# Gate stage's entry: order of token roundings and weight sums; last stage: place of the y and T2 block loads

## The chip, the core and the metric

The kernel runs on one core of a Trainium2 chip. The metric is the device time of one execution in microseconds; for the kernel before, the median of three runs is 1006.84 us (1005.92 to 1007.14). The core has TensorE (PE, matmuls into PSUM), VectorE (DVE), ScalarE (ACT), GpSimd (POOL) and SyncE (SP), whose queue issues most of the DMA transfers. Each engine works through its own queue in order; engines wait for each other with semaphores.

## The reference

`x` is 2048 tokens of 640 features. The result is `x` plus a Fourier mixing of the normalized tokens plus a gated feed-forward layer on them, all in fp32:

```python
xn = _layernorm(x, axis=-1)
a = jnp.einsum("bsd,ed->bse", xn, dft_hid_re)
b = jnp.einsum("bsd,ed->bse", xn, dft_hid_im)
y = jnp.einsum("ts,bse->bte", dft_seq_re, a) - jnp.einsum("ts,bse->bte", dft_seq_im, b)
gate = jnp.einsum("bsd,df->bsf", xn, W_gate)
up = jnp.einsum("bsd,df->bsf", xn, W_up)
gate = gate * (gate > 0)
return x + y + jnp.einsum("bsf,fd->bsd", gate * up, W_down)
```

The hidden width F is 1728, that is 13 tiles of 128 features and 64 left over.

## The kernel before

**Precision.** Every fp32 operand is split into a rounded high part and the low part that is left. `split` (L198) does it: ScalarE rounds (L199), VectorE subtracts (L200). A product is `mm3`, three matmuls one after the other: high by high (L205), high by low (L206), low by high (L207). So the first of three waits for what ScalarE rounded, the second for the token's low part, the third for the weight's low part.

**Three stages.** The first multiplies the sequence DFT with the normalized tokens (`cb` blocks against `xs_early`, `xs_late`) and ends near 399 us. The second is the gate stage: for each of 13 tiles of features it computes gate and up with a fast matrix scheme of 48 products of weight sums and token sums. The last stage, from about 724 us, projects the hidden values and the first stage's result into the output, in two halves `q` of 1024 tokens, `q = 1` first.

**The gate stage** is written as a list of events with keys. `at(key, f)` enters one, the list is sorted by key, and on each engine the instructions stand in that order, by hand. A tile has a period of 33 keys and its products run over 66, so two tiles overlap. Its steps are in `STEPS`: `mm` is a product (weight group, piece, token operand, bank), `seed` has ScalarE copy one PSUM bank into another (L1094), `snap` has it copy a bank to an `ev` buffer (L196), `add` adds a buffer into a bank on VectorE (L1104), `addout` and `both` are likewise VectorE's (L1109, L1115), `final` applies the gate (L1121).

- *Tokens.* 32 token operands are in `FIRST_USE` with the key of their first product. Each is loaded (`fill_slot`, L839) into `mv`, `r` or `xs_early` and split there by `split_slot`: a rounding on ScalarE and directly after it the low part on VectorE, at one key. For the first 14 that key is at most -18 + 1.1 i, for the others 5.5 ahead of the first use. Tokens in `FLIPPED` change sign (L845, L846).
- *Weights.* A tile's raw weights (`gw`, for odd tiles `st`) go through 23 sums, `SUMS`, each one subtraction or addition of 128x128 (L999). `high` then rounds a group of them on ScalarE (L196) and `low` takes the low part on VectorE (L1075). The sums of the first two tiles have fixed keys and are all VectorE's; those of the second start soon after the first tile's products. From the third tile on `plan_sums` places them: at each key where VectorE works on a PSUM bank it gives GpSimd one sum that is free (`sum_beside`, which lets the sum wait for the VectorE instruction just before); a sum that gets due without such a place goes to VectorE.

**The last stage** is a list of units. `B11`, `T1`, `T2`, `B22`, `T3`, `T4` are seven units each, (name, u); `B21` has two. A unit has the steps `load` (token blocks `rw`, `ro`, by `get`), `fetch` (weights `wt`), `prepare` (subtractions L1526, then the split into `cb`), `run` (matmuls) and a reading of the banks; `drive_last` calls them so that loads stand six units ahead of the matmuls, and `prepare` three. SP, POOL and PE keep this order; VectorE and ScalarE are ordered by the scheduler. T1 works on `B12 - B11`, T2 on `B22 - B12`; `load` fetches the `B22` blocks at certain units of T1 and T2. `get_y` loads the input rows `y` (L1433, 256 KB each) to which `add_y` adds a bank (L1438). B11's banks for outputs 0 and 1 are used on by T2, T1's by B22, so they are read in between. In the first half B11's first five units are computed in the gate stage already.

Of the kernel before, what the change touches and what calls it, by code (L numbers as in the profile page):

```python
# [7 lines left out]
F32 = mybir.dt.float32  # L8
F32R = mybir.dt.float32r
AF = mybir.ActivationFunctionType  # L10
# [16 lines left out]
NF = F // P  # L27
# [78 lines left out]
SPLIT_LEAD, FIRST_SPLIT = 5.5, -18  # L106
# [21 lines left out]
def fnet_reglu_kernel(  # L128
# [712 lines left out]
    def split_slot(o):  # L841
        hi, lo = place[o]
        z = lo.bitcast(F32)
        if o in FLIPPED:
            nc.scalar.activation(hi, z, AF.Copy, scale=-1.0)  # L845
            nc.vector.scalar_tensor_tensor(lo, z, -1.0, hi.bitcast(F32), op0=OP.mult, op1=OP.subtract)  # L846
        else:
            split(hi, lo, z)
# [157 lines left out]
    def plan_sums():  # L1006
# [16 lines left out]
        done = {(1, i): max(PERIOD + key, 5 + key / 20) for i, (key, *_) in enumerate(SUMS)}  # L1023

        def free_at(n, i):
            o, _, a, b = SUMS[i][1:]
            t = PERIOD * n - LOADED
# [5 lines left out]
            if n > 1:  # L1033
# [8 lines left out]
        todo = [(n, i) for n in range(2, NF) for i in range(len(SUMS))]  # L1042
# [96 lines left out]
    for n in range(NF):  # L1139
        k0 = PERIOD * n  # L1140
        at(k0 - LOAD_LEAD if n > 1 else -70 + n * 30, load_tile, n)
        for key, *what in SUMS if n < 2 else ():
            at(max(k0 + key, 5 + key / 20) if n == 1 else k0 + key, sum_step, n, *what)
# [77 lines left out]
    for o, (key, s) in zip(combos[UPPER:], places):  # L1221
        at(key, load_again, o, s)
        at(used[o] - SPLIT_LEAD, split_slot, o)
# [187 lines left out]
    Y_AT = {n: "y0" if i < 8 else "y1" if i < 9 else "y2" for i, n in enumerate("001 101 401 41 01 11 21 31 20 30 000 100 400".split())}  # L1411
    HOMES = {"wts": (0,) * 2 + (1,) * 3 + (2,) * (AHEAD - 4), "lead": (1, 0, 0, 1, 1, 2), "low": (0,) + (1,) * 5}
# [39 lines left out]
    def project(q):  # L1452
# [27 lines left out]
        def unit(name, u, first, last):  # L1480
# [7 lines left out]
            def load():  # L1488
# [3 lines left out]
                ahead = {("T1", 2): 0, ("T1", 4): 1, ("T1", 6): 2, ("T2", 0): 3, ("T2", 2): 4, ("T2", 3): 5, ("T2", 4): 6}.get((name, u))  # L1492
# [144 lines left out]
        for name, us in (("B11", every), ("T1", every), ("T2", every), ("B22", every[:4]), ("T3", every), ("B22", every[4:]), ("T4", every)):  # L1637
            for u in us:
# [147 lines left out]
```

## Time and profile before

| | |
|---|---|
| median of three runs | 1006.84 us |
| profiled execution | 1008.12 us |
| its span, first to last instruction | 1006.3 us |
| TensorE matmul | 994.3 us, 4393 |
| VectorE | 884.8 us |
| ScalarE | 526.1 us |
| GpSimd | 146.1 us |
| DMA | 261.14 MB, mean 259 GB/s |
| granted TensorE clock | 1.000 |

An engine's time is the time in which it was busy. Lines of the profile have the form "engine line operation out<-in", L12 being line 12 of the kernel before. A matmul of 128x512 lasts 0.39 us, but the next begins 0.23 us after it, so they overlap, and TensorE counts as busy through short stalls; starts tell more than busy time. In a timeline the brackets at the end give the idle time of the engine ahead of an instruction and what ended it.

### The profile page before, as it was taken

The page shows a single profiled execution, that of the slowest core. Times are in us where ns is not written, and L with a number is a line of the kernel's source. Part 1 is how long each engine was busy: PE and PEld are TensorE (multiplying, and loading weights), DVE is VectorE, ACT ScalarE, POOL GpSimd, SP SyncE. Part 2 cuts the span into 40 slices and gives each one's busy share as a digit, 9 for nine tenths or more (in the row PEclk, how much of TensorE's full clock was granted, in tenths as well). Part 3 has the DMA queues.
Part 4 walks back from the last instruction along what each step waited for, and adds up shares of the span by engine and source line. Part 5 has one row for each costly group of instructions (what it writes and reads, how often), then busy time and mean ns, then how long its engine had stood idle before and what let it go on. Part 6 is the DMA issues. An engine that isn't in the chain of part 4 may idle for free.

```text
span 1006.3 us, 13555 instructions
## 1 busy us (share of the span) xinstructions
PE 994.3 (99%) x4393; PEld 816.8 (81%) x4393; DVE 884.8 (88%) x1462; ACT 526.1 (52%) x832; POOL 146.1 (15%) x285
## 2 busy tenths in 40 slices
PE   9999999999999999999999999999999999999998
PEld 7888888888888888778888888888777888888886
DVE  7968999999989989998999999997778987679877
ACT  6664444333333555776666666657434454444552
POOL 2000000000000000024444544432000001000001
PEclk9999999999999999999999999999999999999999
DMA  9877894986948867716898998765698779999785
GB/s 330 315 256 266 270 326 152 364 303 202 400 140 294 331 200 249 272 66 193 268 263 247 267 255 260 213 179 154 218 398 273 251 251 335 317 308 329 225 273 167
DMA packets 183671, 261.14 MB, mean 259 GB/s; under 512 B 14944, under 2 KB 127200, under 8 KB 183504
## 3 DMA queue, kind: packets, MB, share of 16 engines
q1 hardware_dynamic: 147200, 208.82, 61.6%
q0 software_dynamic: 10944, 38.44, 12.9%
q10 hardware_dynamic: 25456, 13.01, 4.3%
q8 instruction: 34, 0.56, 0.2%
q14 instruction: 37, 0.30, 0.1%
HBM read 198.34 MB, written 75.94 MB: 273 GB/s over the span
## 4 chain that ended last, share of the span: by engine, by line
PE 72%; DVE 11%; issue 8%; DMA 6%; ACT 2%; SPq 1%; POOL 0%; DVEq 0%; ACTq 0%; POOLq 0%
PE ps L205 23%; PE ps L206 23%; PE ps L207 23%; PE ps L583 3%; DVE cb L200 2%; DVE raw L750 1%; DMA pq<-sb 1%; DMA pl<-in_wd 1%; DVE gw L999 1%; DMA rw<-pq 1%; DMA pq<-sa 1%; PE ps L612 1%; DMA rw<-hd 1%; DVE w L1075 1%; PE ps L1585 1%
## 5 line engine op out<-in xcount | busy, mean ns | idle before, releaser
L206 PE MATMUL ps<-cb,wt 128*128 128x512 f32 (+1 forms) x389 | 151.4, 389 | 1.3 <-DVE cb L200 1.2
L205 PE MATMUL ps<-cb,wt 128*128 128x512 f32 (+1 forms) x389 | 151.0, 388 | 1.0 <-ACT cb L199 1.0
L207 PE MATMUL ps<-cb,wt 128*128 128x512 f32 (+1 forms) x389 | 151.0, 388 | 0.0
L199 ACT ACTIVATE cb<-rw 128x1024 fp32r<-128x1024 f32 (+1 forms) x91 | 86.6, 962 | 79.1 <-PE ps L207 42.6
L199 ACT ACTIVATE cb<-raw 128x1024 fp32r<-128x1024 f32 x64 | 67.7, 1060 | 101.6 <-PE ps L207 65.9
L200 DVE TENSOR_TENSOR cb<-rw,cb 128x1024 fp32r<-128x1024 f32 (+1 forms) x91 | 99.4, 1103 | 18.8 <-ACT cb L199 18.0
L206 PE MATMUL ps<-cb,xs_late 128*128 128x512 f32 x232 | 90.5, 390 | 0.1
L1094 ACT ACTIVATE ps<-ps 128x512 f32<-128x512 f32 x104 | 59.2, 581 | 60.0 <-DVE ps L1104 40.3
L200 DVE TENSOR_TENSOR cb<-raw,cb 128x1024 fp32r<-128x1024 f32 x64 | 78.0, 1220 | 14.3 <-ACT cb L199 14.2
L205 PE MATMUL ps<-cb,xs_late 128*128 128x512 f32 x232 | 90.3, 389 | 0.0
L207 PE MATMUL ps<-cb,xs_late 128*128 128x512 f32 x232 | 90.3, 389 | 0.0
L206 PE MATMUL ps<-cb,xs_early 128*128 128x512 f32 x226 | 88.0, 390 | 0.0
L207 PE MATMUL ps<-cb,xs_early 128*128 128x512 f32 x226 | 87.9, 389 | 0.0
L205 PE MATMUL ps<-cb,xs_early 128*128 128x512 f32 x226 | 87.9, 389 | 0.0
L206 PEld LDWEIGHTS ps<-cb,wt 128*128 128x128 f32 x389 | 73.0, 188 | 17.9 <-DVE cb L200 2.9
L196 ACT ACTIVATE ev<-ps 128x512 f32<-128x512 f32 x117 | 69.9, 597 | 33.2 <-PE ps L207 30.3
L205 PEld LDWEIGHTS ps<-cb,wt 128*128 128x128 f32 x389 | 73.0, 188 | 16.5 <-ACT cb L199 1.4
L207 PEld LDWEIGHTS ps<-cb,wt 128*128 128x128 f32 x389 | 73.0, 188 | 14.8
L1109 DVE TENSOR_TENSOR ev<-ps,ev 128x512 f32<-128x512 f32 x91 | 62.4, 686 | 11.8 <-PE ps L207 10.8
L999 POOL TENSOR_TENSOR gw<-gw 128x128 f32<-128x128 f32 x104 | 48.5, 467 | 134.3 <-DVE gw L999 55.1
L199 ACT ACTIVATE wt<-wt 128x768 fp32r<-128x768 f32 (+5 forms) x60 | 38.4, 646 | 54.1 <-DMA wt<-wparts 53.9
L199 ACT ACTIVATE cb<-tk 128x1024 fp32r<-128x1024 f32 x32 | 33.8, 1060 | 50.1 <-DVE tk L750 24.5
(251 smaller groups left out, 2307.9 us busy)
## 6 DMA issues: line engine op xcount, KB each, us to landing
raw<-in_dft SPq DMA_DIRECT2D x94, 512.0 KB, 6.8
wt<-wparts SPq DMA_DIRECT2D x74, 256.0 KB, 4.9
rw<-hd SPq DMA_DIRECT2D x27, 512.0 KB, 6.7
hd<-ev SPq DMA_DIRECT2D x45, 256.0 KB, 3.6
tok<-r ACTq DMA_DIRECT2D x24, 448.0 KB, 6.0
wt<-wparts SPq DMA_DIRECT2D x27, 384.0 KB, 5.3
rw<-pq SPq DMA_DIRECT2D x19, 512.0 KB, 6.0
wparts<-pw SPq DMA_DIRECT2D x24, 384.0 KB, 4.2
```

The costliest lines, as they stand in the source:

```text
L196: return nc.scalar.activation(o, i, AF.Copy)
L199: nc.scalar.activation(hi, src, AF.Copy)
L200: return nc.vector.tensor_tensor(lo, src, hi.bitcast(F32), op=OP.subtract)
L205: nc.tensor.matmul(ps, wh, mh, start=first, stop=False, skip_group_check=more)
L206: nc.tensor.matmul(ps, wh, ml, start=False, stop=False, skip_group_check=more)
L207: nc.tensor.matmul(ps, wl, mh, start=False, stop=last, skip_group_check=more)
L583: nc.tensor.matmul(E[0, key], xn_part(n * SG + j, d)[v == 1], b[:, int(v == 2), j], start=False, stop=n % NH == NH - 1 and (j, v) == (SG - ...
L612: nc.tensor.matmul(E[c, key], xn_part(j, d)[v == 1], b[c][0][:, int(v == 2), j], start=j == 0 and v == 0, stop=False)
L750: sub = lambda o, i0, i1: nc.vector.tensor_tensor(o, i0, i1, op=OP.subtract)
L999: return (engine or nc.vector).tensor_tensor(operand(n, o), operand(n, a), operand(n, b), op=OP.add if op == "+" else OP.subtract)
L1094: nc.scalar.activation(banks[n, x], banks[n, s], AF.Copy, scale=float(sign))
L1109: tt(t, banks[n, x], snaps[n, s], op=OP.add if op == "+" else OP.subtract)
```

## The change

It has three parts. In the gate stage a token's rounding and its low part become two events: `high_slot` stands 2 keys ahead of `low_slot`, and the keys are in a table, `SPLITS`, in place of the rule. The second tile's sums are placed by `plan_sums` too, with the limit that none starts earlier than 28 keys ahead of its tile (38 for later tiles). In the last stage's first half the `B22` blocks are fetched at other units (`ROWS_AHEAD`), B11's banks are read after the last unit of T1 and T1's after the fourth of T2 (`READ_AFTER`), and their y are loaded with T1's last and T2's second unit (`Y_BEFORE`).

```diff
-SPLIT_LEAD, FIRST_SPLIT = 5.5, -18
+SPLITS = {20: -18.5, 38: -18.4, 26: -19.8, 21: -14.7, 22: -15.1, 23: -19.5, 39: -10.9, 28: -14.3, 24: -8.2, 25: -8.1, 42: -7.0, 27: -5.9, 29: -4.3, 30: -3.7, 31: 21.5, 35: 24.5, 32: 26.5, 33: 28.0, 34: 29.5, 36: 34.5, 37: 33.5, 40: 30.5, 41: 37.5, 43: 40.0, 44: 42.5, 45: 46.5, 46: 49.5, 47: 56.5}
+ROUND_AHEAD = 2.0
...
-    def split_slot(o):
+    def high_slot(o):
+        hi, lo = place[o]
+        nc.scalar.activation(hi, lo.bitcast(F32), AF.Copy, scale=-1.0 if o in FLIPPED else 1.0)
+
+    def low_slot(o):
         hi, lo = place[o]
         z = lo.bitcast(F32)
         if o in FLIPPED:
-            nc.scalar.activation(hi, z, AF.Copy, scale=-1.0)
             nc.vector.scalar_tensor_tensor(lo, z, -1.0, hi.bitcast(F32), op0=OP.mult, op1=OP.subtract)
         else:
-            split(hi, lo, z)
+            nc.vector.tensor_tensor(lo, z, hi.bitcast(F32), op=OP.subtract)
...
-        done = {(1, i): max(PERIOD + key, 5 + key / 20) for i, (key, *_) in enumerate(SUMS)}
+        done = {(0, i): key for i, (key, *_) in enumerate(SUMS)}
...
-            t = PERIOD * n - LOADED
+            t = PERIOD * n - (LOADED if n > 1 else 28)
...
-        todo = [(n, i) for n in range(2, NF) for i in range(len(SUMS))]
+        todo = [(n, i) for n in range(1, NF) for i in range(len(SUMS))]
...
-        at(min(used[o] - SPLIT_LEAD, FIRST_SPLIT + 1.1 * i), split_slot, o)
+        at(SPLITS[o] - ROUND_AHEAD, high_slot, o)
+        at(SPLITS[o], low_slot, o)
...
+    ROWS_AHEAD = ({("T1", 2): 0, ("T1", 4): 1, ("T1", 6): 2, ("T2", 0): 3, ("T2", 2): 4, ("T2", 3): 5, ("T2", 4): 6},
+                  {("T1", 3): 0, ("T1", 5): 1, ("T2", 0): 2, ("T2", 1): 3, ("T2", 2): 4, ("T2", 4): 5, ("T2", 5): 6})
+    READ_AFTER = {(1, "B11"): ("T1", 6), (1, "T1"): ("T2", 3)}
+    Y_BEFORE = {(1, "T1", 6): "B11", (1, "T2", 1): "T1"}
...
-                    step.append((l, p, r, (lambda name: lambda: read(name))(kind) if last else idle, f))
-                loaded = "B11" if q and (name, u) == ("T1", 2) else name if u == (5 if q and name == "T1" else 3) and (q, name) != (1, "B11") else None
+                    done = [n for n in ((kind,) if last else ()) if (q, n) not in READ_AFTER] + [n for (k, n), at in READ_AFTER.items() if k == q and at == (kind, i)]
+                    step.append((l, p, r, (lambda names: lambda: [read(n) for n in names])(done), f))
+                loaded = Y_BEFORE.get((q, name, u), name if u == 3 and (q, name) not in READ_AFTER else None)
```

The table for `q = 0` in `ROWS_AHEAD` is the one of before. How instructions move is shown at three places, with the line numbers of each kernel.

**VectorE, from the first tile's products on,** between two adds into a bank (`ps`). `gw<-gw`, `gw<-st` and the like are weight sums, `st` being the second tile's raw weights; `r1` is a token's low part, `w3` and `wb` those of weight groups. Before:

```order
L1104 TENSOR_TENSOR ps_3288<-ps_3288,ev6_3501 128x512
L999 TENSOR_TENSOR gw_3296<-gw_3296,st_3332 128x128
L999 TENSOR_TENSOR gw_3296<-st_3332,gw_3296 128x128
L200 TENSOR_TENSOR r1_2757<-r1_2757 128x512 x2
L999 TENSOR_TENSOR gw_3296<-gw_3296 128x128
L999 TENSOR_TENSOR gw_3296<-gw_3296,st_3332 128x128
L1075 TENSOR_TENSOR wb_3537<-gw_3296,wb_3537 128x384
L999 TENSOR_TENSOR gw_3296<-st_3332 128x128
L1075 TENSOR_TENSOR w3_3546<-gw_3296,w3_3546 128x384
L999 TENSOR_TENSOR gw_3296<-st_3382,st_3332 128x128
L999 TENSOR_TENSOR gw_3296<-gw_3296 128x128
L1104 TENSOR_TENSOR ps_3291<-ps_3291,ev2_3563 128x512
```

The same piece of the changed kernel:

```order
L1112 TENSOR_TENSOR ps_3288<-ps_3288,ev6_3496 128x512
L852 TENSOR_TENSOR r1_2757<-r1_2757 128x512 x2
L1007 TENSOR_TENSOR gw_3296<-gw_3296,st_3332 128x128
L1007 TENSOR_TENSOR gw_3296<-st_3332,gw_3296 128x128
L1007 TENSOR_TENSOR gw_3296<-st_3332,st_3383 128x128
L1083 TENSOR_TENSOR wb_3529<-gw_3296,wb_3529 128x384
L1083 TENSOR_TENSOR w3_3538<-gw_3296,w3_3538 128x384
L1007 TENSOR_TENSOR gw_3296<-st_3332 128x128
L1112 TENSOR_TENSOR ps_3291<-ps_3291,ev2_3553 128x512
```

Seven sums stand between the adds before and four now. Back to the low part of the first tile's second weight group it is 18 and 7; from the second add to the next such add, 3 and 7. Of the second tile's 23 sums, nine are GpSimd's now and 14 VectorE's; of the third tile's, GpSimd has 13 in place of 19.

**ScalarE, right behind,** from the copy `ev2` that the second add above reads to the copy `ev3` of another bank. `ps<-ps` are seeds, the second of which reads the bank of that add; `r1` are token roundings, `w3` and `w1` weight roundings. Before:

```order
L196 ACTIVATE ev2_3563<-ps_3288 128x512
L1094 ACTIVATE ps_3292<-ps_3287 128x512
L1094 ACTIVATE ps_3289<-ps_3291 128x512
L199 ACTIVATE r1_2757<-r1_2757 128x512
L1174 ACTIVATE ev4_3585<-ps_3293 64x512
L196 ACTIVATE w3_3595<-gw_3296 128x384
L196 ACTIVATE w1_3600<-gw_3296 128x128
L199 ACTIVATE r1_2757<-r1_2757 128x512
L196 ACTIVATE ev1_3606<-ps_3287 128x512
L196 ACTIVATE w3_3608<-gw_3296 128x384
L199 ACTIVATE r1_2757<-r1_2757 128x512
L196 ACTIVATE ev3_3616<-ps_3289 128x512
```

The same piece of the changed kernel:

```order
L197 ACTIVATE ev2_3553<-ps_3288 128x512
L844 ACTIVATE r1_2757<-r1_2757 128x512
L1102 ACTIVATE ps_3292<-ps_3287 128x512
L1102 ACTIVATE ps_3289<-ps_3291 128x512
L1182 ACTIVATE ev4_3580<-ps_3293 64x512
L844 ACTIVATE r1_2757<-r1_2757 128x512
L197 ACTIVATE w3_3593<-gw_3296 128x384
L197 ACTIVATE w1_3598<-gw_3296 128x128
L844 ACTIVATE r1_2757<-r1_2757 128x512
L197 ACTIVATE ev1_3604<-ps_3287 128x512
L197 ACTIVATE w3_3606<-gw_3296 128x384
L197 ACTIVATE ev3_3612<-ps_3289 128x512
```

Three roundings stand between the second seed and `ev3` before, two now, and one stands ahead of the seeds. Further on, one rounding fewer stands ahead of the seed for the second tile's product at key 45. At the stage's start ten token roundings stand ahead of the first weight rounding in place of eight.

**SP, in the last stage's first half,** from the loads for T1's fourth unit on (`rw<-hd1` pairs and `ro` are token blocks, `rw<-pq3` of 128x1024 is a `B22` block, `wt` weights). Before:

```order
L1433 DMA y001_6878<-in_xt 128x512
L1433 DMA y101_6880<-in_xt 128x512
L1433 DMA y41_6882<-in_xt 128x512
L1433 DMA y401_6884<-in_xt 128x512
L1504 DMA wt_6892<-wparts_96 128x2x384
L1476 DMA rw_6894<-hd1_93 128x2x512
L1476 DMA rw_6896<-hd1_93 128x2x512
L1504 DMA wt_6922<-wparts_96 128x384
L1472 DMA ro_6924<-hd1_93 128x512
L1474 DMA rw_6926<-pq3_91 128x1024
L1472 DMA ro_6928<-hd1_93 128x512
L1504 DMA wt_6948<-wparts_96 128x2x384
```

The changed kernel:

```order
L1518 DMA wt_6876<-wparts_96 128x2x384
L1490 DMA rw_6878<-hd1_93 128x2x512
L1488 DMA rw_6880<-pq3_91 128x1024
L1490 DMA rw_6882<-hd1_93 128x2x512
L1518 DMA wt_6890<-wparts_96 128x384
L1486 DMA ro_6892<-hd1_93 128x512
L1486 DMA ro_6894<-hd1_93 128x512
L1518 DMA wt_6920<-wparts_96 128x2x384
L1490 DMA rw_6922<-hd1_93 128x2x512
L1488 DMA rw_6924<-pq3_91 128x1024
L1518 DMA wt_6950<-wparts_96 128x2x384
L1490 DMA rw_6952<-hd1_93 128x2x512
```

The four y stood ahead of all of this, with the first `B22` block; two more y stood ahead of the loads for T1's last unit. Now the four follow behind the last row shown, and the two behind T2's first weights and blocks. On VectorE the four adds to these y stand behind the preparation of T1's last unit and T2's first two, where before they stood ahead of T1's fourth unit; the first matmul of T2 waits for one of them and its seventh for another.

More of the change, by code (lines that the diff above doesn't have):

```diff
@@ L1141, in fnet_reglu_kernel @@
         at(k0 - LOAD_LEAD if n > 1 else -70 + n * 30, load_tile, n)
-        for key, *what in SUMS if n < 2 else ():
-            at(max(k0 + key, 5 + key / 20) if n == 1 else k0 + key, sum_step, n, *what)
+        for key, *what in SUMS if n < 1 else ():
+            at(k0 + key, sum_step, n, *what)
         for g, what in enumerate(WEIGHTS):
@@ L1222, in fnet_reglu_kernel @@
         at(key, load_again, o, s)
-        at(used[o] - SPLIT_LEAD, split_slot, o)
+        at(SPLITS[o] - ROUND_AHEAD, high_slot, o)
+        at(SPLITS[o], low_slot, o)
     assert len(places) >= len(combos) - UPPER, (len(places), len(combos))
@@ L1491, in load @@
                     get(kind, u)
-                ahead = {("T1", 2): 0, ("T1", 4): 1, ("T1", 6): 2, ("T2", 0): 3, ("T2", 2): 4, ("T2", 3): 5, ("T2", 4): 6}.get((name, u))
+                ahead = ROWS_AHEAD[q].get((name, u))
                 if ahead is not None:
```

5 lines of the change are left out of this document (4 added, 1 removed).

## Prediction

> **What bounds the kernel now.** I read the page first, then stretches of 50 us, then who waited for whom on TensorE, then the timeline at the waits.
>
> ```profile
> PE 994.3 (99%) x4393; PEld 816.8 (81%) x4393; DVE 884.8 (88%) x1462; ACT 526.1 (52%) x832; POOL 146.1 (15%) x285
> 400.00:450.00 50.00, 47.44 (x200) 36.54 (x199) 46.71 (x105) 37.55 (x75) 4.97 (x11) 1.00 0.50 171
> 600.00:650.00 50.00, 50.00 (x221) 41.22 (x220) 46.69 (x114) 33.60 (x69) 23.27 (x46) 1.00 0.87 241
> 700.00:750.00 50.00, 47.86 (x208) 38.37 (x207) 37.17 (x53) 20.31 (x32) 2.72 (x5) 1.00 0.78 283
> 750.00:800.00 50.00, 49.55 (x218) 40.39 (x217) 45.17 (x52) 24.25 (x31) 0.00 (x0) 1.00 0.82 271
> ```
>
> TensorE is busy 99% of the span, at a granted clock of 1.00 (the third figure from the end of a stretch). A stretch that waits for nothing holds 221 matmuls in 50 us, one every 0.226 us. The change adds and removes no matmul, so it can only win stalls. They lie where the count falls short: 200 in the stretch in which the gate stage begins (21 short, 4.7 us), 208 and 218 where the last stage begins (16 short, 3.6 us). That is the ceiling, some 8 us of 1006.
>
> ```profile
> PE ps L205 <- ACT ev L196: 1.4, 1, 1.4
> PE ps L205 <- ACT ps L1094: 1.2, 3, 0.7
> PE ps L206 <- DVE cb L200: 1.2, 2, 0.8
> PE ps L205 <- ACT cb L199: 1.0, 1, 1.0
> PE ps L205 <- DVE ps L1115: 0.6, 2, 0.3
> ```
>
> The releasers are ScalarE and VectorE: a bank's copy (L196) and seed (L1094), an add into a bank (L1115), and in the last stage the two halves of a token block (L199, L200). At the places themselves (start, duration, matmul):
>
> ```profile
> 425.28 0.39 PE L207 MATMUL ps<-mv,w 128*128 128x512 f32 x1
> 427.04 0.50 PE L205 MATMUL ps<-r,w 128*128 128x512 f32 x1 [1.38 <-ACT ev L196]
> 427.38 0.40 PE L206 MATMUL ps<-r,w 128*128 128x512 f32 x1
> 429.67 0.39 PE L207 MATMUL ps<-r,w 128*128 128x512 f32 x1
> 430.76 0.50 PE L205 MATMUL ps<-r,wa 128*128 128x512 f32 x1 [0.71 <-ACT ps L1094]
> 439.53 0.39 PE L207 MATMUL ps<-mv,w 128*128 128x512 f32 x1
> 439.89 0.50 PE L205 MATMUL ps<-mv,w 128*128 128x512 f32 x1
> 441.85 0.40 PE L207 MATMUL ps<-mv,w 128*128 128x512 f32 x1
> 442.55 0.50 PE L205 MATMUL ps<-xs_early,w 128*128 128x512 f32 x1 [0.31 <-DVE ps L1115]
> ...
> 746.27 0.39 PE L207 MATMUL ps<-cb,wt 128*128 128x512 f32 x1
> 747.68 0.51 PE L205 MATMUL ps<-cb,wt 128*128 128x512 f32 x1 [1.02 <-ACT cb L199]
> 748.94 0.50 PE L206 MATMUL ps<-cb,wt 128*128 128x512 f32 x1 [0.75 <-DVE cb L200]
> 754.97 0.39 PE L205 MATMUL ps<-cb,wt 128*128 128x512 f32 x1
> 755.75 0.50 PE L206 MATMUL ps<-cb,wt 128*128 128x512 f32 x1 [0.40 <-DVE cb L200]
> 759.74 0.39 PE L205 MATMUL ps<-cb,wt 128*128 128x512 f32 x1
> 760.17 0.50 PE L206 MATMUL ps<-cb,wt 128*128 128x512 f32 x1
> ```
>
> A stall costs start minus the start before, less 0.23, and 0.11 more because the matmul after a restart follows at 0.34 (427.04 to 427.38). So in the gate entry 1.53, 0.86, 0.13 and 0.47, and 0.11 each: **3.4 us** in four stalls. In the last stage 1.18, 1.03, 0.55, 0.20 and three times 0.11: **3.3 us**.
>
> **The gate entry, part by part.** Rows of ScalarE and VectorE ahead of the stall of 1.53 us:
>
> ```profile
> 419.55 0.60 ACT L196 ACTIVATE ev<-ps 128x512 f32<-128x512 f32 x1
> 422.08 0.58 ACT L1094 ACTIVATE ps<-ps 128x512 f32<-128x512 f32 x1 [1.19 <-DVE ps L1104]
> 426.40 0.59 ACT L196 ACTIVATE ev<-ps 128x512 f32<-128x512 f32 x1
> 426.88 1.15 ACT L199 ACTIVATE r<-r 128x512 fp32r<-128x512 f32 x2
> ...
> 421.35 0.69 DVE L1104 TENSOR_TENSOR ps<-ps,ev 128x512 f32<-128x512 f32 x1
> 429.34 0.69 DVE L1104 TENSOR_TENSOR ps<-ps,ev 128x512 f32<-128x512 f32 x1
> 447.08 0.48 DVE L999 TENSOR_TENSOR gw<-gw 128x128 f32<-128x128 f32 x2
> ```
>
> TensorE waits for the copy at 426.40, ScalarE stood idle 1.19 us for the add at 421.35, and that add stood behind VectorE's sums. A sum takes VectorE 0.20 us (a second one makes 0.48 of 0.28). Between the low part of the second weight group and this add stand 18 sums before and 7 now (the second tile's other sums come later or go to GpSimd): 11 x 0.20 = 2.2 us less, which would put the add at 419.15. Its other input, the copy at 419.55, is ready at 420.15, so the add starts there, 1.2 us sooner. ScalarE now puts a token's rounding (0.52 each: two in 1.15) into the idle time, and the two seeds follow; the second can start at 420.15 + 0.52 less an overlap, and one seed of 0.49: about 421.07. From that seed to the copy ScalarE had 4.32 us without a gap (422.08 to 426.40); one rounding fewer stands there now, so 3.8: copy at 424.87, done 425.46. TensorE asks for it at 425.28 + 0.23 = 425.51. The stall of 1.53 + 0.11 goes, with 0.05 us to spare.
>
> What is late next: the add at 429.34, which feeds the seed for 430.76 (1.42 us later). Before, 7.99 us lay between the two adds, 1.6 of it waiting for roundings. Four more sums stand there now (0.8) and the waits for roundings should go: 7.99 - 1.6 + 0.8 = 7.2, from 420.15: 427.3, so the bank at 428.7. TensorE, which now keeps its pace, asks at 425.51 + 12 x 0.227 = 428.23. The stall falls from 0.86 to about 0.4; I take 0.5 us won. The stall of 0.13 (and 0.11) at 439.89 waits for a seed on ScalarE with one rounding of 0.52 fewer in front: it goes, 0.24. The stall of 0.47 at 442.55 follows an add on VectorE, in front of which the postponed sums now stand; I leave it as it is.
>
> Gate entry: 1.64 + 0.5 + 0.24 = **2.4 us**. Moving ten token roundings ahead of the first weight rounding costs nothing: VectorE, full there, takes the same low parts, and ScalarE has idle time. The first weights' low part comes one low part (0.6) sooner, but the second group's has the same work in front and pins TensorE at the same time, so I count nothing.
>
> The unknown cost is nine sums of the second tile on GpSimd beside a full VectorE. Rows of the two together, a little later:
>
> ```profile
> 440.24 1.07 POOL L999 TENSOR_TENSOR gw<-gw 128x128 f32<-128x128 f32 x2 [5.49 <-DVE wa L1075]
> 441.21 0.68 DVE L846 SCALAR_TENSOR_TENSOR xs_early<-xs_early 128x512 fp32r<-128x512 f32 x1
> ```
>
> Two sums cover 440.24 to 441.31, and VectorE's operation that begins inside (441.21) still takes its 0.68. Bounds: nothing (this row), or nine times a sum of about 0.5 held up in full, 4.5 us of VectorE time. I take nothing, the row being of this very pair. The Trainium skill, "SBUF — State Buffer", Who interferes with whom, says that a VectorE instruction with two SBUF inputs and a GpSimd instruction that reads SBUF block each other fully. By that page the gate entry would win nothing wherever the sums slip off the PSUM adds they are set beside; the row at 441.21, whose two inputs are in SBUF, shows no such hold of 0.5.
>
> **The last stage.** The queue of SP carries y and the blocks; the columns of the first row are start, time and count:
>
> ```profile
> 730.78 4.45 SPq L1433 DMA_DIRECT2D y<-in_xt  x4
> 745.23 1.23 DVE L1526 TENSOR_TENSOR rw<-rw 128x1024 f32<-128x1024 f32 x1 [0.85 <-DMA rw<-hd]
> 740.00:745.00 5.00, 5.00 (x24) 4.14 (x23) 3.55 (x6) 1.20 (x2) 0.00 (x0) 1.00 1.05 405
> y<-in_xt SPq DMA_DIRECT2D x9, 256.0 KB, 6.5
> 739.52 1.28 DVE L1438 TENSOR_TENSOR y<-ps,y 128x512 f32<-128x512 f32 x2
> ```
>
> The DMA engines are full (share 1.05) at 405 GB/s, and the subtraction at 745.23 waits for a block. Four y (4 x 262 KB = 1.05 MB, 2.6 us) no longer stand ahead of it: it lands at 742.6. TensorE's second matmul came 748.94 - 745.23 = 3.71 us after the landing: now 746.3, and it is asked for at 746.27 + 0.45 = 746.7. Both stalls there go. The blocks behind it shed all six y, 1.57 MB or 3.9 us; the later two stalls need 1.18 + 1.03 + 0.11 + 0.66 = 3.0 and 3.3 us. They go too, by 0.9 and 0.6 us.
>
> The reads of B11's banks (four adds of 0.60 on VectorE, 739.52) move to the end of T1, and T2's first product waits for one of them, its seventh matmul for another: a new wait. Behind the adds on VectorE stand the halves of T2's third block. Walking VectorE's new order from the subtraction at 742.6 with 1.14 per 128x1024 operation, 0.60 per 128x512, 0.87 and 0.47 per weight half, I get the two reads done at 759.6 and 760.2; the four y land by 750 + 4 x 0.65 = 752.6, ahead of their turn. T2 starts at 760.17 + 0.34 + 16 x 0.227 - 3.3 = 760.8, the seventh matmul at 762.2. Cover of 1.2 us; without it each us late is a us of TensorE. At B22's first unit the weight halves now queue behind a block that waits for a buffer: between 0 and one weight half (0.87); I take 0.2, since my walk ends 0.1 from need. Last stage: 3.3 - 0.2 = **3.1 us**.
>
> Sum: 2.4 + 3.1 = 5.5 us. The profiled execution took 1008.12 us (span 1006.3 and 1.8 around it), so it would take 1002.6. The median shown is 1006.84, 0.13% lower; stalls are the same there, so 1006.84 - 5.5 = **1001.3**.
>
> **The rivals.**
> - Gate entry won only in part: the postponed sums (8 x 0.20 = 1.6 us) meet the add before 442.55, or GpSimd holds VectorE. For it: only 0.05 us to spare at the first stall, VectorE 46.71 busy of 50. Against: VectorE's waits for roundings vanish. Then 0.8 + 3.1: 1002.9.
> - The last stage won only in part: the y adds on VectorE delay T1's last blocks and T2's first. For: slacks of 0.5 to 1.2 us. Against: the same adds leave the place before the first stall. Then 2.4 + 1: 1003.4.
> - The change does not do what it says: the third tile gives back six sums to VectorE for the nine taken, so only three leave it, and stalls move on instead of going; in the last stage VectorE, not the DMA, sets the pace. Then about 1006.8.
> - Slower: T2's first product waits for y at the end of a full queue. Price: every us beyond 1.2. It outweighs the rest from 5.5 + 2.0 + 1.2 = 8.7 us late, y landing at 761.3: the 6.3 MB from 736 on at 250 GB/s instead of 405. The stretch's 405 speaks against. Then 1009. The Trainium skill, "DMA: Bandwidth & Descriptors", Where 436 GB/s comes from, lets HBM bind at about 358 GB/s; by it y would come some 2 us later than at 405, still not enough, and the measured 405 decides.
> - Better: the stall at 442.55 and the small ones ahead of 420 go as well: 999.5.
>
> **How the numbers follow.** Forecast 0.52 (its own range 1000.4 to 1002.2), gate in part 0.20, last stage in part 0.12, nothing 0.07, slower 0.04, better 0.05. The range 1000.0 to 1004.3 holds the forecast, the first rival, over half of the second and a little of "better": about 0.8. Faster by over 0.2% (2.0 us, about what a measurement of this kernel can tell from no change): 0.52 + 0.20 + 0.12 + 0.05, less 0.01 for the weak end of the second rival: 0.88. Same 0.08, slower 0.04.
>
> **What would show it.** Right: some 217 matmuls or more in the 50 us of the gate entry, no wait of TensorE for a copy (L196 before) there; none for block halves between 740 and 765; subtraction of the block pair near 740 (742.6 less the gate's 2.4); T2's first matmul not held by an add to y. Wrong: a new wait of L205 for an add of y, GpSimd rows stretched beyond 0.5 us with VectorE rows stretched beside them, or the stall of 0.47 grown past 1 us.

## The result and the profile after

The changed kernel takes **1001.84 us**, the median of four runs (1000.28 to 1002.88), against 1006.89 for the kernel before beside it (1005.92 to 1007.14): a ratio of 0.995, 95% interval 0.9933 to 0.9968, so 3.2 to 6.7 us less. The forecast was 1001.3, with a range of 1000.0 to 1004.3. The profiled execution of the changed kernel was its fastest run (1000.28, span 998.5), that of before was above its median (1008.12): the 7.8 us between the two profiles aren't the change's alone, as the experiments show.

In the changed kernel the three product lines of TensorE are L206 to L208 (before L205 to L207), ScalarE copies a bank at L197, seeds at L1102 and rounds tokens at L844, VectorE adds into a bank at L1112 and L1123, takes low parts at L852, sums at L1007 and adds to y at L1452. First the page's busy line of the changed kernel:

```profile
PE 992.9 (99%) x4393; PEld 818.4 (82%) x4393; DVE 883.0 (88%) x1459; ACT 525.7 (53%) x832; POOL 147.0 (15%) x288
```

Then three of its stretches of 50 us (busy time and count of TensorE, weight loads, VectorE, ScalarE, GpSimd, then clock, share of the DMA engines, GB/s):

```profile
400.00:450.00 50.00, 50.00 (x218) 40.00 (x217) 47.14 (x104) 38.80 (x78) 8.34 (x18) 1.00 0.52 179
700.00:750.00 50.00, 49.63 (x218) 40.42 (x217) 39.67 (x51) 23.01 (x34) 2.40 (x5) 1.00 0.85 310
750.00:800.00 50.00, 49.84 (x220) 40.95 (x219) 42.02 (x50) 20.95 (x27) 0.00 (x0) 1.00 0.84 278
```

200, 208 and 218 matmuls have become 218, 218 and 220, of about 221 that fit. VectorE is as busy as before: what changed is the order in which it does its work. The places themselves in its timeline (start, duration, instruction), TensorE at the former stalls of the gate entry, then at the one stall that is new:

```profile
424.61 0.39 PE L208 MATMUL ps<-mv,w 128*128 128x512 f32 x1
424.83 0.45 PE L206 MATMUL ps<-r,w 128*128 128x512 f32 x1
427.43 0.39 PE L208 MATMUL ps<-r,w 128*128 128x512 f32 x1
427.68 0.50 PE L206 MATMUL ps<-r,wa 128*128 128x512 f32 x1
438.57 0.40 PE L208 MATMUL ps<-mv,w 128*128 128x512 f32 x1
438.88 0.50 PE L206 MATMUL ps<-xs_early,w 128*128 128x512 f32 x1
...
772.81 0.39 PE L207 MATMUL ps<-cb,wt 128*128 128x512 f32 x1
773.36 0.50 PE L208 MATMUL ps<-cb,wt 128*128 128x512 f32 x1 [0.16 <-DVE wt L201]
773.69 0.39 PE L206 MATMUL ps<-cb,wt 128*128 128x512 f32 x1
```

The matmul that waited 1.53 us for a copy now follows 0.22 after the one before it; the one that waited 0.86 for a seed follows at 0.25. The former stall of 0.47 (442.55 before) is 0.08 at 438.88. New is 0.32, and 0.10 at the restart, at 773.36: a weight half of B22's first unit. ScalarE, VectorE and GpSimd at the gate entry show why:

```profile
424.15 0.59 ACT L197 ACTIVATE ev<-ps 128x512 f32<-128x512 f32 x1
414.38 0.70 DVE L1112 TENSOR_TENSOR ps<-ps,ev 128x512 f32<-128x512 f32 x1
416.43 1.29 DVE L852 TENSOR_TENSOR r<-r 128x512 fp32r<-128x512 f32 x2 [1.35 <-ACT r L844]
419.51 0.69 DVE L1112 TENSOR_TENSOR ps<-ps,ev 128x512 f32<-128x512 f32 x1
426.27 0.68 DVE L1112 TENSOR_TENSOR ps<-ps,ev 128x512 f32<-128x512 f32 x1
414.42 0.45 POOL L1007 TENSOR_TENSOR gw<-st 128x128 f32<-128x128 f32 x1 [20.82 <-DVE ev L1183]
```

The add starts at 419.51 instead of 421.35, and VectorE even has time to wait 1.35 us for a rounding ahead of it; the copy ends at 424.74, 0.09 us before TensorE's 424.83. The second add is 6.76 us behind the first (7.99 before). In the last stage, SP's queue and VectorE:

```profile
737.44 2.63 SPq L1447 DMA_DIRECT2D y<-in_xt  x4
737.04 1.22 DVE L1540 TENSOR_TENSOR rw<-rw 128x1024 f32<-128x1024 f32 x1 [1.06 <-DMA rw<-hd]
748.78 0.68 DVE L1452 TENSOR_TENSOR y<-ps,y 128x512 f32<-128x512 f32 x1
752.78 1.88 DVE L1452 TENSOR_TENSOR y<-ps,y 128x512 f32<-128x512 f32 x3
771.21 1.22 DVE L201 TENSOR_TENSOR cb<-rw,cb 128x1024 fp32r<-128x1024 f32 x1 [0.94 <-ACT cb L200]
772.35 2.29 DVE L201 TENSOR_TENSOR wt<-wt 128x768 fp32r<-128x768 f32 x3
```

The pair's block is subtracted at 737.04 instead of 745.23, before the y are even requested, and no block half is waited for between 740 and 765. The weight half of 772.35 stands behind a block for whose rounding VectorE waits (0.94 us). That this block waits for a buffer, as the prediction had it, isn't shown: ScalarE's rounding of it begins at 770.12 after 1.37 us of idle time, for which the profile names no releaser.

### The profile page after: what moved, and what is told of

Read it like the earlier page. It is cut to its first block, busy times and chain, and to the rows that moved or that the text cites. A ratio compares the mean times of both kernels' runs of the same rounds, so it can differ in the third digit from the quotient of the medians.

```text
span 998.5 us, 13547 instructions
## 1 busy us (share of the span) xinstructions
PE 992.9 (99%) x4393; PEld 818.4 (82%) x4393; DVE 883.0 (88%) x1459; ACT 525.7 (53%) x832; POOL 147.0 (15%) x288
## 4 chain that ended last, share of the span: by engine, by line
PE 95%; DVE 3%; issue 1%; DMA 1%; ACT 0%; SPq 0%; DVEq 0%; ACTq 0%
PE ps L207 30%; PE ps L206 30%; PE ps L208 30%; PE ps L584 3%; PE ps L613 1%; PE ps L1599 1%; DMA pl<-in_wd 1%; PE ps L185 1%; DVE ev L1117 1%; DVE ev L1129 0%; DVE w L1083 0%; DVE gw L1007 0%; DVE wt L201 0%; DVE ps L1112 0%; DVE pw L1282 0%
## 5 line engine op out<-in xcount | busy, mean ns | idle before, releaser
L208 PE MATMUL ps<-cb,wt 128*128 128x512 f32 (+1 forms) x389 | 151.0, 388 | 0.2 <-DVE wt L201 0.2
L207 PE MATMUL ps<-cb,wt 128*128 128x512 f32 (+1 forms) x389 | 151.0, 388 | 0.1
L206 PE MATMUL ps<-cb,wt 128*128 128x512 f32 (+1 forms) x389 | 150.9, 388 | 0.0
L207 PE MATMUL ps<-cb,xs_late 128*128 128x512 f32 x232 | 90.6, 390 | 0.0
L206 PE MATMUL ps<-cb,xs_late 128*128 128x512 f32 x232 | 90.3, 389 | 0.0
L208 PE MATMUL ps<-cb,xs_late 128*128 128x512 f32 x232 | 90.3, 389 | 0.0
L1102 ACT ACTIVATE ps<-ps 128x512 f32<-128x512 f32 x104 | 59.2, 581 | 56.3 <-DVE ps L1112 37.2
L207 PE MATMUL ps<-cb,xs_early 128*128 128x512 f32 x226 | 88.0, 390 | 0.0
L206 PE MATMUL ps<-cb,xs_early 128*128 128x512 f32 x226 | 87.9, 389 | 0.0
L208 PE MATMUL ps<-cb,xs_early 128*128 128x512 f32 x226 | 87.9, 389 | 0.0
L197 ACT ACTIVATE ev<-ps 128x512 f32<-128x512 f32 x117 | 70.0, 598 | 33.4 <-PE ps L208 31.6
L207 PEld LDWEIGHTS ps<-cb,wt 128*128 128x128 f32 x389 | 73.0, 188 | 15.6 <-DVE cb L201 0.5
L208 PEld LDWEIGHTS ps<-cb,wt 128*128 128x128 f32 x389 | 73.0, 188 | 15.4 <-DVE wt L201 0.6
L206 PEld LDWEIGHTS ps<-cb,wt 128*128 128x128 f32 x389 | 73.0, 188 | 15.2
L1007 POOL TENSOR_TENSOR gw<-gw 128x128 f32<-128x128 f32 x101 | 47.0, 465 | 95.4 <-DVE wa L1083 25.1
```

Of the source, the lines that this page charges most:

```text
L197: return nc.scalar.activation(o, i, AF.Copy)
L206: nc.tensor.matmul(ps, wh, mh, start=first, stop=False, skip_group_check=more)
L207: nc.tensor.matmul(ps, wh, ml, start=False, stop=False, skip_group_check=more)
L208: nc.tensor.matmul(ps, wl, mh, start=False, stop=last, skip_group_check=more)
L1007: return (engine or nc.vector).tensor_tensor(operand(n, o), operand(n, a), operand(n, b), op=OP.add if op == "+" else OP.subtract)
L1102: nc.scalar.activation(banks[n, x], banks[n, s], AF.Copy, scale=float(sign))
```

## The experiments

Theory A is the prediction's: two independent gains, each by the terms of its sum. The kernel before was timed again in each of three comparisons (c1 to e2, e3 to e6, e7 to e10), with medians of 1007.87, 1007.98 and 1007.09 us. The table gives each kernel's ratio to its own, the gain worked out from it, and TensorE's stalls in its one profile by place (start less the start before, less 0.227, plus what the restart costs the next matmul). Two places are kept apart because they turn out to be chance: 406 to 412, and 495 to 500. Some 1.3 us at 675, 709 and 724 and 0.3 at 414 to 418 stand in nearly all and are left out, as are single ones of at most 0.6 us elsewhere. An interval reaches 1 to 2 us to either side; where two expectations lie closer than that, the text decides by the stalls, which are those of one profile each.

| kernel | ratio (95% interval) | gain, us | 406-412 | gate 424-445 | 495-500 | 742-760 | 773 |
|---|---|---|---|---|---|---|---|
| before (first profile) | | | 0.69 | 3.54 | 0.62 | 3.29 | 0 |
| c1, before again | 1.0001 (0.9991-1.001) | 0 | 0.19 | 3.56 | 0.68 | 2.40 | 0 |
| after (first profile) | 0.995 (0.9933-0.9968) | 5.0 | 0 | 0.43 | 0 | 0 | 0.42 |
| c2, after again | 0.9935 (0.9921-0.9948) | 6.6 | 0 | 0.43 | 0.93 | 0 | 0.42 |
| e1, gate alone | 0.9961 (0.9948-0.9974) | 3.9 | 0 | 0.45 | 0.40 | 2.78 | 0 |
| e2, last stage alone | 0.9971 (0.9961-0.9982) | 2.9 | 0 | 3.50 | 0.85 | 0 | 0.42 |
| e3, roundings alone | 0.9968 (0.9956-0.998) | 3.2 | 0.51 | 1.75 | 0 | 3.11 | 0 |
| e4, sums alone | 0.9984 (0.9972-0.9996) | 1.6 | 0 | 2.34 | 0.62 | 2.55 | 0 |
| e5, after, blocks early | 0.9938 (0.9926-0.9951) | 6.2 | 0.20 | 0.45 | 0 | 0 | 1.04 |
| e6, after, y early | 0.996 (0.9945-0.9974) | 4.0 | 0.59 | 0.45 | 0.96 | 2.01 | 0 |
| e7, after, no lead | 0.9956 (0.9944-0.9969) | 4.4 | 0.41 | 1.55 | 0.86 | 0 | 0.42 |
| e8, after, no GpSimd | 0.9961 (0.9947-0.9975) | 3.9 | 0.51 | 1.25 | 0.99 | 0 | 0.42 |
| e9, after, y later | 0.9966 (0.9953-0.9978) | 3.4 | 0.38 | 0.46 | 0.67 | 1.36 | 0.42 |
| e10, after, two moves | 0.9938 (0.9925-0.9952) | 6.2 | 0.06 | 0.44 | 1.11 | 0 | 0.42 |

**c1 and c2: both kernels once more**, without an edit.

> The kernel before once more, unchanged, as a measure of what one profile differs from another by itself. Theory A (the gate entry's stalls belong to the order of work): the time is the same within 0.2%, and the profile again shows the stalls of TensorE at 406.7 and 411.8 (together 0.7 us), 427.0 (1.6), 430.8 (1.0), 439.9 (0.2), 442.6 (0.6), some 5 us between 400 and 500, and 3.3 us between 745 and 762. Rival C (a part of what went between the two profiles is chance): in the first stage a token's transfer that ScalarE waits for near 374 lands about 1.3 us sooner or later from one execution to the next, VectorE reaches the weights of the gate entry that much sooner or later, and the stalls at 406.7 and 411.8 come and go with it, so that the 400 to 450 stretch shows more than 203 matmuls in this run if VectorE's block operation near 376 starts by 375.3.

> The changed kernel once more, unchanged. Theory A: 5.0 us less than the kernel before (3.5 to 6.5), TensorE's stalls from 390 us on about 2.6 us in all, none of them for a copy near 427 or for block halves between 740 and 765, one of some 0.4 us at the first weight half of the B22 units near 773. Rival C: where VectorE's block operation near 376 starts late (376.4 instead of 375.2), the stalls at 406.7 and 411.8 are back in part (0.3 to 0.7 us) and so is a part of the one at 427, since the change left that one only some 0.05 us to spare.

The kernel before has the same time and the same stalls between 424 and 445 (3.56 us), the changed one the same absence of them. But two other places differ between profiles of one kernel. In the first stage, whose order is the same in all, a block of VectorE begins in the profile of before, behind a token for which ScalarE waited, at

```profile
374.88 0.63 ACT L199 ACTIVATE xs_early<-xs_early 128x512 fp32r<-128x512 f32 x1 [1.13 <-DMA xs_early<-tok]
376.49 1.23 DVE L200 TENSOR_TENSOR cb<-raw,cb 128x1024 fp32r<-128x1024 f32 x1 [1.26 <-ACT cb L199]
```

in c1 at

```profile
376.31 1.23 DVE L200 TENSOR_TENSOR cb<-raw,cb 128x1024 fp32r<-128x1024 f32 x1
```

and in e2, with the gate entry of before too, at

```profile
375.38 1.23 DVE L200 TENSOR_TENSOR cb<-raw,cb 128x1024 fp32r<-128x1024 f32 x1
```

The stalls at 406 to 412 are 0.69, 0.19 and 0 us in these three. Rival C was right on them: they are there in the changed gate entry of e3, e6 and e8 (0.5 to 0.6) and absent from the unchanged one of e2. What counts is how far this block is ahead of TensorE, whose first product of the gate stage starts at 399.12, 399.45 and 398.88 in the three: 22.6, 23.1 and 23.5 us. Over the fourteen profiles, with either gate entry, a lead of 23.3 us or more leaves no stall (five profiles), and from 23.2 down to 22.6 us the stall grows from 0.06 to 0.69 (nine). Rival C was wrong on the stall at 427: both runs with the whole old order have it again, c1 and e2, and e6 with the changed entry doesn't, though its block begins as late as 377.54. (495 to 500 is the second such place; e10 below.)

**e1 and e2: each half alone.** e1 takes all of the change that comes ahead of the last stage (roundings and sums), e2 the rest, of which the core is:

```diff
+    READ_AFTER = {(1, "B11"): ("T1", 6), (1, "T1"): ("T2", 3)}
+    Y_BEFORE = {(1, "T1", 6): "B11", (1, "T2", 1): "T1"}
...
-                ahead = {("T1", 2): 0, ("T1", 4): 1, ("T1", 6): 2, ("T2", 0): 3, ("T2", 2): 4, ("T2", 3): 5, ("T2", 4): 6}.get((name, u))
+                ahead = ROWS_AHEAD[q].get((name, u))
```

> The kernel before with the gate entry's part of the change alone (roundings two steps ahead of the low parts, the second tile's sums planned). Theory A as predicted: 2.4 us less than before, 1004.4. Theory B (the gate entry won more than its three stalls, since the low parts of the first two weight groups and the third tile's seeds come sooner as well): 2.4 + 0.7 + 0.4 + 0.6 = 4.1 us less, 1002.7. In both the last stage keeps its stalls of 3.3 us near 747 to 760.

> The kernel before with the last stage's part of the change alone (y and the token blocks of B22 loaded later, two reads of y moved back). Theory A: 3.1 us less than before, 1003.7; theory B, which takes the gate entry at 4.1, leaves 0.9 to 2.9 us for it, 1004.0 to 1005.9 (5.0 measured in all less 4.1, up to the stalls in the profile: 3.29 less the new 0.42). In both the gate entry keeps its stalls, and a new one of 0.2 to 0.5 us stands where B22's first unit waits for a weight half.

3.9 and 2.9 us, together 6.8, where the whole gave 6.6 on the same chip: within the noise the halves are independent. The gate's stalls between 424 and 445 fall by 3.1, more than the 2.4 of theory A and less than the 4.1 of theory B, two of whose terms (406 to 412 and 495 to 500) are the places of chance. By the time alone (3.9, from 2.6 to 5.2) theory B could stand. The last stage loses 2.4 to 3.3 us of stalls and gains the 0.42 at 773.

**e3 and e4: the gate's two parts.** e3 has the new steps of roundings and low parts and the old 23 sums; e4 the planned sums and the old splitting, of which the core is:

```diff
-        todo = [(n, i) for n in range(2, NF) for i in range(len(SUMS))]
+        todo = [(n, i) for n in range(1, NF) for i in range(len(SUMS))]
```

> The kernel before with the roundings of the tokens two steps ahead of their low parts, and nothing else: the second tile's 23 sums stay on VectorE in their old places. Theory A (VectorE's sums set the add ahead of the stall at 427.0, ScalarE's roundings set VectorE's later waits): the add stays near 421 and its seeds with it, only one rounding of 0.52 us leaves ScalarE's way to the copy, so the stall of 1.64 falls to about 1.1; VectorE's waits of 1.65 us for roundings go, and with them the stall of 0.97 at 430.8 and 0.24 at 439.9. 1.7 us less than before, 1005.1 on a median of 1006.8. Rival D (the roundings do it all; the sums were covered): 3.3 us or more less, and no stall above 0.3 us between 420 and 450.

> The kernel before with the second tile's sums planned (put off, some on GpSimd), and nothing else: tokens are split as before. Theory A: the add comes 1.2 us sooner, so the stall at 427.0 falls from 1.64 to about 0.4; the waits for roundings stay, so the stalls of 0.97 at 430.8 and 0.24 at 439.9 stay. 1.2 us less than before. Rival E (the sums do it all): 3.3 us or more less. Rival D: within 0.4 us of before.

TensorE in e3, then in e4:

```profile
427.09 0.50 PE L206 MATMUL ps<-r,w 128*128 128x512 f32 x1 [0.84 <-ACT ev L197]
429.73 0.39 PE L208 MATMUL ps<-r,w 128*128 128x512 f32 x1
430.22 0.50 PE L206 MATMUL ps<-r,wa 128*128 128x512 f32 x1
```

```profile
427.11 0.50 PE L205 MATMUL ps<-r,w 128*128 128x512 f32 x1 [0.22 <-ACT ev L196]
430.30 0.50 PE L205 MATMUL ps<-r,wa 128*128 128x512 f32 x1 [0.18 <-ACT ps L1094]
442.68 0.50 PE L205 MATMUL ps<-xs_early,w 128*128 128x512 f32 x1 [0.91 <-DVE ps L1115]
```

With the restart, e3's first stall is 1.10 (expected 1.1), its second 0.37 (expected gone); in all 1.8 us less in the gate, 1.7 expected. e4's first stall is 0.48 (expected 0.4). Its total of 1.2 us less is the expected one, but from two errors: the second stall fell to 0.44 where it should have stayed at 0.97, and the one near 442 grew from 0.58 to 1.18. There the postponed sums meet the add, the mechanism of the prediction's first rival. With the roundings ahead as well it is 0.18. So neither part does it all: E falls by e4's time as well (1.6 us, at most 2.8), D by the stalls alone, since e3's time (3.2, from 2.0 to 4.4) would allow it. And the roundings take away the harm that the sums do alone.

**e5 and e6: the last stage's two parts.** In e5 B22's blocks are requested in the old places and y late; in e6 y and its reads are in the old places and the blocks late:

```diff
-                ahead = ROWS_AHEAD[q].get((name, u))
+                ahead = ROWS_AHEAD[0].get((name, u))
```

> The changed kernel with B22's token blocks requested in their old places, so that of the last stage's change only y's part is left. Theory A (four y, 1.05 MB, stood ahead of the block pair): all of the last stage's gain is here, no stall of block halves between 740 and 765, and the time is that of the changed kernel within 0.5 us, 5.0 to 6.4 less than before; the stall of 0.42 us at B22's first weight half may be there or not. Rival F (B22's blocks, 0.52 MB each, stood in the way as well): 0.6 to 1.6 us more than the changed kernel, with block halves late again near 743 to 757.

> The changed kernel with y loaded and read in its old places, so that of the last stage's change only the later requests of B22's token blocks are left. Theory A: y still stands ahead of the pair, so the stalls of the last stage are there as in the kernel with the gate's part alone, 2.4 to 2.8 us between 740 and 757; 3.8 us less than before. Rival F: one block of 0.52 MB (1.3 us at 405 GB/s) no longer stands ahead of the pair, and it lands that much sooner: the stalls fall by half, to about 1.3 us, and the time is 5 us less than before.

TensorE in e5, then in e6:

```profile
774.11 0.50 PE L208 MATMUL ps<-cb,wt 128*128 128x512 f32 x1 [0.77 <-DVE wt L201]
```

```profile
745.00 0.50 PE L206 MATMUL ps<-cb,wt 128*128 128x512 f32 x1 [0.32 <-ACT cb L200]
746.30 0.50 PE L207 MATMUL ps<-cb,wt 128*128 128x512 f32 x1 [0.80 <-DVE cb L201]
```

y's part alone removes every stall of block halves, as theory A has it, but pays 1.04 at 773. The blocks' part alone leaves 2.0 us of them and has nothing at 773; the third of them (0.66 in before) is gone, so a little of rival F holds. So y carries the gain and makes the new wait, and the later blocks bring that from 1.04 to 0.42. In times e5 can't be told from the whole.

y's part moves two things, the requests of y and the four adds on VectorE. The subtraction of the block pair in e1, then in e5, which differ by y's part alone:

```profile
740.86 1.23 DVE L1536 TENSOR_TENSOR rw<-rw 128x1024 f32<-128x1024 f32 x1 [0.76 <-DMA rw<-hd]
```

```profile
736.93 1.23 DVE L1540 TENSOR_TENSOR rw<-rw 128x1024 f32<-128x1024 f32 x1 [0.20 <-DMA rw<-hd]
```

In e1 VectorE was through with the adds and idle for 0.76 us when the pair landed, so what held the subtraction there was the landing, and not the adds.

**e7: the lead of the roundings.** `ROUND_AHEAD = 0.0`.

> The changed kernel with each token's rounding directly ahead of its low part instead of two steps ahead (the low parts keep their new steps). Theory A: VectorE waits for a rounding again at each low part of a token, as in the kernel that has the sums' part alone, and TensorE has the stalls of that run between 425 and 445 (0.44, 0.44, 0.24 and 1.18 us) in place of its 0.4: about 1.5 to 2 us more than the changed kernel. Rival G (the new steps of the low parts carry the gain, not the two steps of lead): within 0.5 us of the changed kernel.

1.1 us of stalls come back in the gate (0.43 to 1.55), 0.50 of it for a seed at 428.75, 0.71 for the add at 440.81; the stall for the copy does not. Between the two expectations: the new steps of the low parts carry most of the roundings' gain, the lead of two steps the rest.

**e8: the second tile's sums back on VectorE.**

```diff
-        at(key, sum_beside if near else sum_step, n, *SUMS[i][1:])
+        at(key, sum_beside if near and n > 1 else sum_step, n, *SUMS[i][1:])
```

> The changed kernel with the second tile's nine sums on GpSimd given back to VectorE, at the same places of the plan. Theory A (GpSimd's sums hold nothing up, and VectorE is full there): one sum of 0.20 us stands ahead of the add at 419.5 and three more ahead of the one at 426.3, so a stall of about 0.2 us comes back near 425 and one of about 0.5 near 428, and the one of 0.18 near 439 grows by two sums more: 0.7 to 1.5 us more than the changed kernel. Rival H (the two engines hold each other up on their common memory): nine times 0.46 less 0.20, 2.3 us less than the changed kernel. Rival I (the sums on GpSimd were never needed): within 0.3 us.

0.8 us of stalls come back (0.43 to 1.25), inside theory A's 0.7 to 1.5:

```profile
430.25 0.50 PE L206 MATMUL ps<-r,wa 128*128 128x512 f32 x1 [0.41 <-ACT ps L1102]
```

That is 0.57 and 0.11 at the second stall, where 0.5 was expected. Rival H falls by the time (3.9 us, where it had some 8), I by the stalls: GpSimd's share is worth 0.8 us.

**e9: the slower rival made on purpose.**

```diff
-    Y_BEFORE = {(1, "T1", 6): "B11", (1, "T2", 1): "T1"}
+    Y_BEFORE = {(1, "T2", 2): "B11", (1, "T2", 1): "T1"}
```

> The changed kernel with the four y of B11's reads requested three units later (at T2's unit 2 instead of T1's unit 6). This is the slower rival of the prediction, made on purpose. They are then issued near 750 to 752.7 and land some 6.7 us later, the third near 758.1; its add is done near 758.8, and T2's first product, which needs it, would start at 756.9. Theory A: a stall of 1.9 us (1 to 3.5) there, for an add to y, and the time 2 us above the changed kernel's, 4.4 less than before. Rival J (the add isn't what T2 waits for, or the cover is larger than 1.2 us): within 0.4 us of the changed kernel.

VectorE and TensorE at T2's start:

```profile
756.42 1.28 DVE L1452 TENSOR_TENSOR y<-ps,y 128x512 f32<-128x512 f32 x2
757.62 0.67 DVE L1540 TENSOR_TENSOR ro<-ro 64x512 f32<-64x512 f32 x1
758.22 2.47 DVE L1452 TENSOR_TENSOR y<-ps,y 128x512 f32<-128x512 f32 x4
...
759.00 0.47 PE L206 MATMUL ps<-cb,wt 128*128 128x512 f32 x1 [1.12 <-issue]
```

T2's first product starts 0.1 us after the first of the four adds ends (758.22 + 0.68), 1.28 late: the price of 1 us for 1 us holds, and the time goes with it (a gain of 3.4). But the cause isn't the transfer: the four adds run without a gap at 0.60 each, so every y had landed, and the add waits only for its turn behind VectorE's other work: requested later, it got a later place there, behind the two adds of T1's y (756.42). The profile names no releaser here ("issue"); the add that ends just before tells. In the changed kernel that add ends at 752.78 + 0.60 + 0.68 = 754.1 (the second of the three). T2's first matmul, the one that starts at 759.00 in e9, starts at 756.27 there, without a wait: a cover of 2.2 us, not 1.2.

**e10: two more moves.** B22's first unit splits its weights ahead of its block, and a leading token's split goes behind the add of key 46.6:

```diff
-LEADS = ((12, (24, 26)), (22, (34, 36)), (29, (40,)), (38, (45, 47)), (46.5, (52,)))
+LEADS = ((12, (24, 26)), (22, (34, 36)), (29, (40,)), (38, (46.65, 47)), (46.5, (52,)))
...
+                    early = (q, name, u) == (1, "B22", 0)
+                    if early:
+                        split(w[:, :, 0], w[:, :, 1], w[:, :, 1].bitcast(F32))
```

> The changed kernel with two more moves. B22's first unit in the last stage splits its weights ahead of its token block, so that the weight halves no longer queue behind a block that waits for its buffer: the stall of 0.42 us near 773 goes. In the last gate tile the split of one leading token (key 45) moves behind the add of key 46.6, so that this add starts at about 706.5 instead of 708.05: the stall of 0.56 us near 708.8 goes. Theory A: both go, 0.98 us less than the changed kernel, 7.4 less than before. Rival K: the low parts that were put off (0.7 us later) or the block behind the weights are late in their turn, and a new stall of 0.3 us or more stands within 10 us of either place: within 0.4 us of the changed kernel.

The second move worked: the stall of 0.56 near 708.8 is gone, and none stands behind it. The first had no effect: ScalarE and VectorE have the same order as without it, since the last stage writes out the order of SP, GpSimd and TensorE alone and leaves theirs to the scheduler; so 0.42 us stand at 775.64 as in the changed kernel. The time doesn't decide: 6.2 us, from 4.8 to 7.6, holds the changed kernel's gain as well as the expected 7.4. In the profiled run, the slowest of the five, 1.11 us stand at 498.28:

```profile
489.16 0.29 DVE L1306 TENSOR_TENSOR pw<-pl 128x128 f32<-128x128 f32 x1 [1.54 <-DMA pl<-in_wd]
497.64 0.58 ACT L1102 ACTIVATE ps<-ps 128x512 f32<-128x512 f32 x1 [3.96 <-DVE ps L1112]
498.28 0.50 PE L206 MATMUL ps<-r,wa 128*128 128x512 f32 x1 [0.85 <-ACT ps L1102]
```

VectorE waits 1.54 us for a transfer of 128 KB, and everything behind it, the seed of 497.64 too, is late. In c2 that wait was 1.04 and the stall 0.93, in c1 0.77 and 0.68; in the first profile of after VectorE waited for no such transfer and there was no stall. Over the fourteen profiles VectorE waits for it in eleven, and the stall is that wait less 0.1 (in e10 less 0.4); in the other three (after, e3, e5) there is neither.

## Why the prediction was right

- **Gate entry, the stall of 1.53 + 0.11 at 427.04: right, with its margin.** Gone, with 0.09 us to spare (0.05 predicted). The add came at 419.51, not 420.15, because the copy that was to bind it was sooner too, as was TensorE itself, which had no stall at 406 to 412 in this profile. e3 and e4 show both steps by themselves: the sums 1.2 us, the rounding 0.5.
- **The stall at 430.76: mechanism right, size short.** 0.5 of 0.97 was to be won, 0.86 was. The second add came 6.76 us after the first instead of 7.2. The four more sums stand there as predicted (0.8), so 7.99 - 6.76 + 0.8 = 2.0 us of waits went; the sum had 1.6, the two waits that the view names.
- **The stall at 439.89 (0.24): right,** it is gone; 0.07 stands one product later.
- **The stall at 442.55: the step that failed.** "I leave it as it is" was 0.58; it is 0.18. The sums alone make it 1.18, the roundings alone leave 0.22 in e3: the term lacked what the roundings ahead win there. With the previous one this makes the gate 3.1 us where the sum had 2.4.
- **The first weights' low parts: rightly counted at nothing.** Their low part came 0.85 us sooner behind the block of 376 (28.7 us behind it in after, 29.6 before; 0.6 predicted), that of the second group 0.1. The stalls vanished in the profile of after, but come and go with both gate entries, by the lead of that block.
- **GpSimd beside VectorE: the value held, the row didn't carry it.** No sum in the gate entry was stretched, and e8 prices their place at 0.8 us. But the row on which the zero rested overlaps the sums by 0.1 us only (441.21 to 441.31), too little to show a hold. What decides is what VectorE does beside the sum; the last section has the rows.
- **Last stage, 3.1 us: right but for a size that varies.** The pair is subtracted at 737.04 ("near 740"), all block halves are in time, y is the cause (e5, e6). Its first term was short: the pair was to land 2.6 us sooner, by y's bytes; from e1 to e5 it is 3.9, of which 0.5 is TensorE's earlier start of the stage. The stalls removed are 2.4 to 3.3 us over five profiles with y in its old place and the blocks in theirs, because the pair's landing varies: the first matmul waits 0.3 to 1.2 us, while the second always follows 1.03 late, VectorE's half behind ScalarE's. The new wait at B22 was taken as 0.2 inside 0 to 0.87, and is 0.42. Net 2.0 to 2.9.
- **The cover of T2: right in kind, short in size:** 2.2 us, not 1.2, and its end is set by the add's turn on VectorE, not by y's landing.
- **The sum.** 3.1 + (2.0 to 2.9) = 5.1 to 6.0 us by the stalls; 5.0 and 6.6 by two comparisons; 5.5 predicted. Between the two first profiles lie 7.8 us: 1.3 more are the places of chance (0.69 + 0.62), and 0.4 lie behind the last matmul, from whose start to the span's end it is 4.4 us in the profile of before and 4.0 in that of after. It is 4.0 in e1 and all kernels made from the changed one, and 4.2 to 4.5 in the others; why stays open, and the prediction had no term for it.

## What to carry to other kernels

Where TensorE is busy to 99%, count its starts: each stall has a price, and the parts of a change add up by it. Before a stall is put down to a change, look whether a second profile of the same kernel still has it; one that hangs on a transfer's landing comes and goes. And judge two parts together as well as apart: postponed work that harms by itself (1.18 us) may be harmless beside a change that empties the engine.

## What the runs showed of the hardware

Two transfers land at times that differ between executions whose order up to there is the same: the token near 374 us (VectorE's block behind it begins between 375.0 and 377.9 over the fourteen profiles) and the 128 KB of `pl` near 486 (VectorE waits 0 in the first profile of after and 1.04 us in c2). They cost TensorE 0 to 0.7 and 0 to 1.1 us over the fourteen profiles, at most 1.55 together in one (e6). The first stage varies by more: TensorE's first product of the gate stage starts between 398.4 (c2) and 401.1 us (e4), though every engine's order is the same up to 385 us in all of them. The four runs of the changed kernel differ by 2.6 us.

A sum on GpSimd does hold up a VectorE operation where both of VectorE's inputs are in SBUF. In the timeline of after, GpSimd and VectorE:

```profile
519.47 0.46 POOL L1007 TENSOR_TENSOR gw<-gw,st 128x128 f32<-128x128 f32 x1 [1.07 <-DVE pw L1275]
519.55 0.79 DVE L1083 TENSOR_TENSOR w<-gw,w 128x384 fp32r<-128x384 f32 x1
```

and the group of that operation from 450 to 680 us (busy time, then the mean in ns):

```profile
L1083 DVE TENSOR_TENSOR w<-gw,w 128x384 fp32r<-128x384 f32 x73 | 40.4, 554 | 0.5 <-ACT w L197 0.5
```

The low part takes 0.79 us instead of its mean of 0.554 and ends 0.41 after the sum, as if it had hardly begun before. In e1 it takes 0.80 us beside the same sum. The add at 414.38, one of whose inputs is in PSUM, takes its 0.70 beside the sum at 414.42. The Trainium skill, "SBUF — State Buffer", Who interferes with whom, lets a VectorE instruction with two inputs in SBUF and a GpSimd one that reads SBUF shut each other out, and one with a single input there not; both rows agree. The plan sets each sum of the gate stage beside an operation that reads PSUM: 146 of GpSimd's 152 sums in after take 0.45 to 0.47 us. The other six take 0.54 to 0.96, all near a transfer that GpSimd issues itself; their cause stays open.
